# Loading x already transposed through the DMA crossbar instead of transposing it on TensorE

## The chip, the cores and the metric

One core of a Trainium2 chip runs the kernel. The metric is device microseconds (us) from the first to the last instruction of an execution, with the launch's small overhead; "span" is the same without it, as a profile shows it (about 1.8 us less: 289.9 of 291.7 in the profiled run of the kernel before). Each kernel was run several times, beside runs of the kernel before on the same chip. The engines are written as in the profile: PE is TensorE's matmuls, PEld its weight loads, DVE VectorE, ACT ScalarE, POOL GpSimd; SPq and ACTq are the queues on which SyncE and ScalarE issue transfers (the "sync queue" and the "second queue" below).

## The reference

x is 2048 x 512 in bf16. The result mixes a sliding-window attention (32 heads of 16, window 256) and a gated feed-forward block (inner size 1376), with a sigmoid gate per row.

```python
x = A_x
g = sigmoid((x * gate_w).sum(-1, keepdims=True))
a = attention(x @ wqkv, window=256) @ wo      # 32 heads of 16, causal, banded
b = (silu(x @ w1) * (x @ w3)) @ w2
return g * a + (1 - g) * b
```

Every product that contracts over the 512 columns of x needs x with those columns on the partitions, that is, x transposed (`xT` below).

## The kernel before

x is loaded in four pieces of 512 rows, row-major, and TensorE transposes it in 128x128 blocks into PSUM; ScalarE and VectorE take turns to copy the blocks out.

```python
def x_dma(t):
    xs = xp.tile([P, 4, D], BF16, name="xs")
    nc.sync.dma_start(out=xs[:], in_=x2d[512 * t:512 * (t + 1), :].rearrange("(m p) d -> p m d", p=P))
    xs_tiles[t] = xs

x_dma(0); w_dma(D, 2 * D); w_dma(0, D); x_dma(1); w_dma(2 * D, 3 * D)    # K, Q, V weights
...
def x_transposes(m2):                       # 256 rows
    tx = gen.tile([P, 2, NDC, P], BF16, name="g")
    for j in range(2):
        ...
        for c in range(NDC):
            nc.tensor.transpose(out=tx[:, j, c, :], in_=xs[:, m % 4, c * P:(c + 1) * P], identity=ident[:])
    dst = xT[:, :, 2 * m2 * P:(2 * m2 + 2) * P].rearrange("p c (j t) -> p j c t", j=2)
    if m2 % 2 == 0:
        nc.scalar.copy(out=dst, in_=tx[:])
    else:
        nc.vector.tensor_copy(out=dst, in_=tx[:])
```

TensorE's order is fixed by the program. There are 92 "score bursts" (score matmuls for one block, then exp on ScalarE). Units with a fixed place (`must`) follow a burst, and feed-forward units fill the rest of a time budget, which is kept in estimated microseconds:

```python
COST = {"proj": 0.87, "v": 0.87, "tx": 0.45, "gate": 0.4, "up": 0.87, "down": 2.38, "out": 0.87, "pv": 1.22}
...
must[0] += [("v", proj_v, (0,)), ("v", proj_v, (1,)), ("tx", x_transposes, (2,)), ("tx", x_transposes, (3,))]
...
def run(unit):
    kind, fn, args = unit
    done[0] += COST.get(kind, 0)
    fn(*args)
...
for n, (fn, c, a) in enumerate(bursts):
    fn(c, a)                                         # scores and exp
    before = done[0] - carry
    for unit in early: run(unit)                     # projections, transposes, gate
    while (n >= FFN_FROM and ffn_i[0] < len(up_down) and done[0] + lc - before < QUANTUM - 0.4):
        run_ffn()                                    # feed-forward as filler
    carry = min(done[0] + lc - before - QUANTUM, CARRY)
    for unit in late: ...                            # attention output, projection out
```

Here `lc` is the cost of the burst's `late` units, and `carry` hands what a burst overran its `QUANTUM` by to the next one, at most `CARRY` (1.0).

The softmax here doesn't subtract the row's maximum and nothing guards it: scores larger than these inputs give would overflow.

Of the kernel before, what the change touches and what calls it, by code (L numbers as in the profile page):

```python
# [7 lines left out]
ALU = mybir.AluOpType  # L8
ACT = mybir.ActivationFunctionType
BF16 = mybir.dt.bfloat16  # L10
# [5 lines left out]
P = 128  # L16
# [3 lines left out]
def kernel(  # L20
# [12 lines left out]
    nc = tc.nc  # L33
    x2d = A_x.flatten_outer_dims()
    out2d = out.flatten_outer_dims()
    S, D = x2d.shape
# [4 lines left out]
    NDC = D // P  # L41
# [8 lines left out]
    pp = ctx.enter_context(tc.tile_pool(name="pp", bufs=1))  # L50
    xT = pp.tile([P, NDC, S], BF16, name="xT")
# [1 line left out]
    OT = pp.tile([P, NDC, S], BF16, name="OT")  # L53
    gq = pp.tile([P, NT], F32, name="gq")
    omg = pp.tile([P, NT], F32, name="omg")
    ident = pp.tile([P, P], BF16, name="ident")
    wo_sb = pp.tile([P, NDC, D], BF16, name="wo_sb")
    w2_sb = pp.tile([P, NFC, D], BF16, name="w2_sb")
    bsb = pp.tile([P, NT, D], BF16, name="bsb")
# [3 lines left out]
    wqkv_sb = pp.tile([P, NDC, 3 * D], BF16, name="wqkv_sb")  # L63
# [1 line left out]
    eo = pp.tile([P, 4], F32, name="eo")  # L65
    maskEO = pp.tile([P, 2], F32, name="maskEO")

    xp = ctx.enter_context(tc.tile_pool(name="xp", bufs=2))
    qkpool = ctx.enter_context(tc.tile_pool(name="qk", bufs=2))
    dmpool = ctx.enter_context(tc.tile_pool(name="edm", bufs=5))  # L70
    efpool = ctx.enter_context(tc.tile_pool(name="ef", bufs=3))
# [5 lines left out]
    ssml = ctx.enter_context(tc.tile_pool(name="ssml", bufs=2, space=bass.MemoryType.PSUM))  # L77
    gen = ctx.enter_context(tc.tile_pool(name="gen", bufs=3, space=bass.MemoryType.PSUM))

    xs_tiles = {}  # L80

    def x_dma(t):
        xs = xp.tile([P, 4, D], BF16, name="xs")
        nc.sync.dma_start(out=xs[:],
                          in_=x2d[512 * t:512 * (t + 1), :].rearrange("(m p) d -> p m d", p=P))
        xs_tiles[t] = xs

    def w_dma(lo, hi):
        nc.sync.dma_start(out=wqkv_sb[:, :, lo:hi],
                          in_=A_wqkv[:, lo:hi].rearrange("(c p) f -> p c f", p=P))  # L90

    x_dma(0)
    w_dma(D, 2 * D)
    w_dma(0, D)
    x_dma(1)
    w_dma(2 * D, 3 * D)
    nc.gpsimd.dma_start(out=gwc[:], in_=gate_w.rearrange("(c p) -> p c", p=P))

    nc.gpsimd.memset(ident[:], 0.0)
    nc.gpsimd.affine_select(out=ident[:], in_=ident[:], pattern=[[-1, P]],  # L100
                            compare_op=ALU.not_equal, fill=1.0, base=0, channel_multiplier=1)
    nc.gpsimd.memset(eo[:], 1.0)
    nc.gpsimd.affine_select(out=eo[:], in_=eo[:], pattern=[[-2 * DH, 4]],
                            compare_op=ALU.is_ge, fill=0.0, base=0, channel_multiplier=1)
    nc.gpsimd.affine_select(out=eo[:], in_=eo[:], pattern=[[2 * DH, 4]],
                            compare_op=ALU.is_ge, fill=0.0, base=DH - 1, channel_multiplier=-1)
# [4 lines left out]
    nc.gpsimd.affine_select(out=maskA[:], in_=maskA[:], pattern=[[1, P]],  # L111
                            compare_op=ALU.is_ge, fill=0.0, base=0, channel_multiplier=-1)
    nc.gpsimd.memset(Vaug[:, :, :, DH:DH + 1], 1.0)

    def x_transposes(m2):
        tx = gen.tile([P, 2, NDC, P], BF16, name="g")
        for j in range(2):
            m = 2 * m2 + j
            xs = xs_tiles[m // 4]
            for c in range(NDC):  # L120
                nc.tensor.transpose(out=tx[:, j, c, :], in_=xs[:, m % 4, c * P:(c + 1) * P],
                                    identity=ident[:])
        dst = xT[:, :, 2 * m2 * P:(2 * m2 + 2) * P].rearrange("p c (j t) -> p j c t", j=2)
        if m2 % 2 == 0:
            nc.scalar.copy(out=dst, in_=tx[:])
        else:
            nc.vector.tensor_copy(out=dst, in_=tx[:])  # L127

    qk_tiles = {}

# [167 lines left out]
    for c in range(NDC):  # L298
        for p in range(NP):
            bursts.append((burst_dm, c, 2 * p))  # L300
            bursts.append((burst_dm, c, 2 * p + 1))
            if p < NP - 1:
# [2 lines left out]
    NB = len(bursts)  # L305

    must = {n: [] for n in range(NB + 40)}
    start = [("tx", x_transposes, (0,)), ("tx", x_transposes, (1,)),
             ("proj", proj, (0, 0, False)), ("proj", proj, (0, 0, True))]
    must[0] += [("v", proj_v, (0,)), ("v", proj_v, (1,)), ("tx", x_transposes, (2,)),  # L310
                ("tx", x_transposes, (3,))]
    must[1] += [("proj", proj, (0, 1, False)), ("proj", proj, (0, 1, True))]
    must[2] += [("v", proj_v, (2,)), ("v", proj_v, (3,)), ("gate", gate, (0,))]
    must[3] += [("v", proj_v, (4,)), ("v", proj_v, (5,)), ("tx", x_transposes, (4,))]
    must[4] += [("tx", x_transposes, (5,)), ("proj", proj, (0, 2, False)),
                ("proj", proj, (0, 2, True))]
    must[6] += [("v", proj_v, (6,)), ("v", proj_v, (7,)), ("gate", gate, (1,))]
    must[8] += [("v", proj_v, (8,)), ("tx", x_transposes, (6,)), ("tx", x_transposes, (7,))]
    must[9] += [("v", proj_v, (9,)), ("proj", proj, (0, 3, False)), ("proj", proj, (0, 3, True))]
    must[11] += [("gate", gate, (2,)), ("v", proj_v, (10,))]  # L320
    must[12] += [("v", proj_v, (11,))]
# [37 lines left out]
    with tc.manual_schedule(engines={mybir.EngineType.PE}):  # L359
        alloc_qk(0)  # L360
        for unit in start:
            run(unit)
        nc.sync.dma_start(out=w1_sb[:], in_=B_w1.rearrange("(c p) f -> p c f", p=P))
        nc.sync.dma_start(out=w3_sb[:], in_=B_w3.rearrange("(c p) f -> p c f", p=P))
        x_dma(2)
        x_dma(3)
        nc.sync.dma_start(out=w2_sb[:, 0:NFC - 1, :],
                          in_=B_w2[0:(NFC - 1) * P, :].rearrange("(f p) n -> p f n", p=P))
# [58 lines left out]
```

## Time and profile before

| | before |
|---|---|
| time, median of 40 runs beside the change | 290.4 us (288.6 to 293.6) |
| first score matmul (profiled run) | 13.23 us |
| last score burst (its first weight load) | 270.0 us |

The busy times of the page, then of each engine in single stretches. In a stretch's line the columns are: its bounds and length, then for PE, PEld, DVE, ACT and POOL the busy time and number of instructions, the granted clock, the busy share of the 16 DMA engines and what they moved.

```profile
span 289.9 us, 7509 instructions
PE 258.9 (89%) x3152; PEld 164.6 (57%) x3184; DVE 186.7 (64%) x398; ACT 213.9 (74%) x297; POOL 71.8 (25%) x125
```

```profile
0.00:13.20 13.20, 5.64 (x24) 2.58 (x25) 2.44 (x5) 2.98 (x3) 4.54 (x13) 1.00 0.82 256
...
100.00:150.00 50.00, 46.76 (x605) 30.99 (x608) 33.26 (x76) 40.98 (x60) 12.01 (x20) 1.00 0.04 8
150.00:200.00 50.00, 46.12 (x575) 30.43 (x577) 33.64 (x76) 42.39 (x61) 14.41 (x24) 1.00 0.05 11
```

After the start TensorE (PE) is busy 46 to 47 of 50 us and holds 55% of the chain of work that ended last (ACT 19%, DVE 14%), so most of the time depends on it. In the first 13.2 us it has only 5.6 us of work. (The clock of 1.00 in that line says nothing: the trace's first clock record begins at 19.3 us, and a matmul of 512 columns took up to 0.63 us before it, 0.38 later.) The timeline of PE in the start (start, length, what; in brackets the idle time before it and what ended it):

```profile
4.44 1.89 PE L121 MATMUL g<-ident,xs 128*128 128x128 bf16 x16 [4.44 <-DMA xs<-in_A_x_dram]
7.20 1.86 PE L142 MATMUL g<-xT,wqkv_sb 128*128 128x512 bf16 x4 [0.88 <-DVE xT L127]
9.79 1.89 PE L142 MATMUL g<-xT,wqkv_sb 128*128 128x512 bf16 x4 [0.72 <-DMA wqkv_sb<-in_A_wqkv_dram]
13.23 0.61 PE L226 MATMUL big<-qz,kt 32*128 32x512 bf16 x3 [1.56 <-DVE qz L147]
```

These are the first 16 transposes, the K projection, the Q projection (which waited for its weights) and the first scores. PE's waits that the change is aimed at, over the whole run (us, times, longest):

```profile
PE g L121 <- DMA xs<-in_A_x_dram: 4.4, 1, 4.4
...
PE g L142 <- DVE xT L127: 2.1, 3, 0.9
...
PE g L142 <- DMA wqkv_sb<-in_A_wqkv_dram: 0.7, 1, 0.7
```

The kernel already has one kind of crossbar transpose: 64 of 128x128 from SBUF for the attention output. Their time on the issuing queue (min/median/max in ns) and to landing:

```profile
L281 SPq DMA_TRANSPOSE OT<-ocur x64: 1094/1222/2152, 25.9 to 275.3; - x64
...
DMA to landing us min/median/max: 2.2/2.3/3.5
```

### The profile page before, as it was taken

What the parts mean: (1) busy time and instruction counts of PE and PEld (TensorE: products, weight loads), DVE (VectorE), ACT (ScalarE), POOL (GpSimd) and SP (SyncE); (2) the same over time, 40 slices, a digit from 0 to 9 for tenths busy, and PEclk for the clock granted to TensorE, in tenths of its full rate; (3) what the DMA queues carried; (4) which work ended last, traced back from release to release, by engine and by line L of the source; (5) the groups of instructions that cost most, each with busy time, mean ns of one, the idle gap of its engine ahead of it and who ended that gap; (6) DMA issues with size and microseconds to landing.
All of it is one profiled execution on the core that took longest, in us unless ns stands there. A gap on an engine that the chain in (4) does not pass through costs nothing.

```text
span 289.9 us, 7509 instructions
## 1 busy us (share of the span) xinstructions
PE 258.9 (89%) x3152; PEld 164.6 (57%) x3184; DVE 186.7 (64%) x398; ACT 213.9 (74%) x297; POOL 71.8 (25%) x125
## 2 busy tenths in 40 slices
PE   2699898899989999899998999988998998999994
PEld 2145565555655656566665655675675446655671
DVE  1148566777776666558668775566578666765783
ACT  3158887968968999778778988887888778868220
POOL 6003331133303333212302333330232213333000
PEclk9999999999999999999999999999999999999999
DMA  6997000000000000000000000000001111111101
GB/s 164 374 384 252 11 2 9 14 9 11 11 2 19 11 7 9 9 9 10 12 7 14 11 11 9 11 3 9 11 14 46 31 40 33 48 48 43 44 9 36
DMA packets 19298, 13.10 MB, mean 45 GB/s; under 512 B 10721, under 2 KB 18241, under 8 KB 19265
## 3 DMA queue, kind: packets, MB, share of 16 engines
q1 hardware_dynamic: 19232, 12.63, 14.1%
q8 instruction: 25, 0.41, 0.6%
q0 software_dynamic: 32, 0.00, 0.3%
q14 instruction: 9, 0.07, 0.1%
HBM read 8.42 MB, written 2.10 MB: 36 GB/s over the span
## 4 chain that ended last, share of the span: by engine, by line
PE 55%; ACT 19%; DVE 14%; issue 8%; DMA 3%; SPq 0%; ACTq 0%
PE g L199 13%; PE g L183 12%; PE g L272 9%; ACT edm L216 8%; DVE edm L232 5%; ACT edm L217 5%; PE g L142 5%; PE big L226 5%; PE g L206 4%; PE g L154 4%; ACT ef L216 4%; DMA wqkv_sb<-in_A_wqkv_dram 3%; PE big L245 2%; DVE hT L191 2%; DVE qz L147 2%
## 5 line engine op out<-in xcount | busy, mean ns | idle before, releaser
L252 POOL TENSOR_SCALAR_AFFINE_SELECT ef<-ef 128x512 bf16<-128x512 bf16 x112 | 67.3, 638 | 194.4 <-ACT ef L216 194.4
L216 ACT ACTIVATE edm<-big 128x1536 bf16<-128x1536 f32 x64 | 90.6, 1416 | 29.2 <-PE sml L226 29.1
L183 PE MATMUL g<-xT,w_sb 128*128 128x256 bf16 (+1 forms) x704 | 86.4, 273 | 5.3 <-DVE hT L191 4.9
L183 PEld LDWEIGHTS <-w_sb 128*128 128x128 bf16 (+1 forms) x704 | 66.7, 100 | 23.7 <-issue 14.6
L232 DVE TENSOR_TENSOR edm<-edm,maskA 128x1024 bf16<-128x1024 bf16 x64 | 44.2, 691 | 47.1 <-ACT edm L217 46.9
L216 ACT ACTIVATE ef<-big 128x1536 bf16<-128x1536 f32 x28 | 40.7, 1455 | 11.0 <-PE sml L245 10.6
L199 PE MATMUL g<-w_sb,hT 128*128 128x512 bf16 (+1 forms) x163 | 40.0, 379 | 2.1 <-DVE hT L191 1.1
L187 ACT ACTIVATE tt<-g 128x256 bf16<-128x256 f32 (+1 forms) x88 | 32.7, 395 | 11.3 <-PE g L183 9.8
L272 PEld LDWEIGHTS <-edm 128*128 128x128 bf16 x992 | 38.3, 96 | 4.5 <-issue 2.6
L272 PE MATMUL g<-Vaug,edm 128*128 128x17 bf16 x992 | 40.5, 170 | 0.0
L272 PE MATMUL g<-Vaug,ef 128*128 128x17 bf16 x448 | 36.8, 171 | 1.6 <-DVE hT L191 1.0
L217 ACT ACTIVATE edm<-sml 128x512 bf16<-128x512 f32 x64 | 37.5, 587 | 0.0
L142 PE MATMUL g<-xT,wqkv_sb 128*128 128x512 bf16 x121 | 33.7, 397 | 4.1 <-DVE xT L127 2.1
L272 PEld LDWEIGHTS <-ef 128*128 128x128 bf16 x448 | 34.9, 96 | 3.4 <-issue 1.3
L199 PEld LDWEIGHTS <-hT 128*128 128x128 bf16 (+1 forms) x176 | 17.0, 98 | 20.0 <-issue 2.3
L226 PE MATMUL big<-qz,kt 32*128 32x512 bf16 x192 | 24.8, 381 | 3.6 <-DVE qz L147 1.6
L226 PE MATMUL sml<-qz,kt 32*128 32x512 bf16 x64 | 24.4, 381 | 0.0
L142 PEld LDWEIGHTS <-wqkv_sb 128*128 128x128 bf16 x128 | 10.9, 99 | 19.5 <-issue 7.3
L275 DVE RECIPROCAL rden<-g 128x16 f32<-128x16 f32 x32 | 8.2, 257 | 20.4 <-PE g L272 20.1
L154 PE MATMUL g<-wqkv_sb,xT 128*128 128x512 bf16 x55 | 16.8, 417 | 1.1 <-DVE hT L191 0.7
L217 ACT ACTIVATE ef<-sml 128x512 bf16<-128x512 f32 x28 | 16.8, 601 | 0.0
L206 PE MATMUL g<-wo_sb,OT 128*128 128x512 bf16 x61 | 16.2, 381 | 0.2
(214 smaller groups left out, 231.7 us busy)
## 6 DMA issues: line engine op xcount, KB each, us to landing
w_sb<-in_B_w_dram SPq DMA_DIRECT2D x2, 1376.0 KB, 14.0
xs<-in_A_x_dram SPq DMA_DIRECT2D x4, 512.0 KB, 8.0
out_dram<-ot SPq DMA_DIRECT2D x16, 128.0 KB, 1.7
wqkv_sb<-in_A_wqkv_dram SPq DMA_DIRECT2D x3, 512.0 KB, 7.9
w_sb<-in_B_w_dram SPq DMA_DIRECT2D x1, 1280.0 KB, 14.6
OT<-ocur SPq DMA_TRANSPOSE x64, 2.3
wo_sb<-in_A_wo_dram SPq DMA_DIRECT2D x1, 512.0 KB, 7.6
w_sb<-in_B_w_dram SPq DMA_DIRECT2D x1, 96.0 KB, 7.1
```

The costliest lines, as they stand in the source:

```text
L142: nc.tensor.matmul(ps[:], lhsT=wqkv_sb[:, dc, col0:col0 + P], rhs=xT[:, dc, t0:t1], start=(dc == 0), stop=(dc == NDC - 1))
L154: nc.tensor.matmul(ps[:], lhsT=xT[:, c, m * P:(m + 1) * P], rhs=wqkv_sb[:, c, 2 * D:3 * D], start=(c == 0), stop=(c == NDC - 1))
L183: nc.tensor.matmul(gu[0:fs, wch, :], lhsT=wsb[:, dc, f * P:f * P + fs], rhs=xT[:, dc, t * 256:(t + 1) * 256], start=(dc == 0), stop=(dc == ...
L187: nc.scalar.activation(out=tt[0:fs, :], in_=gu[0:fs, 0, :], func=ACT.Tanh, scale=0.5)
L199: nc.tensor.matmul(ps[:], lhsT=hT[0:fs, f, (m % 2) * P:(m % 2 + 1) * P], rhs=w2_sb[0:fs, f, :], start=(f == 0), stop=(f == NFC - 1))
L206: nc.tensor.matmul(ps[:], lhsT=OT[:, c, m * P:(m + 1) * P], rhs=wo_sb[:, c, :], start=(c == 0), stop=(c == NDC - 1))
L216: nc.scalar.activation(out=dst[:, 0:3, 0:w], in_=big[:, :, 0:w], func=ACT.Exp, scale=SCALE)
L217: nc.scalar.activation(out=dst[:, 3, 0:w], in_=sml[:, 0:w], func=ACT.Exp, scale=SCALE)
L226: nc.tensor.matmul(dst, lhsT=kt[32 * u:32 * u + 32, kb * P:(kb + 1) * P], rhs=qz[32 * u:32 * u + 32, :, kb * P:kb * P + n], start=True, st ...
L232: nc.vector.tensor_tensor(out=tri, in0=tri, in1=maskA[:, None, None, :].to_broadcast([P, 4, 2, P]), op=ALU.mult)
L252: nc.gpsimd.affine_select(out=tri, in_=tri, pattern=[[0, 4], [-1, P]], compare_op=ALU.is_ge, fill=0.0, base=-1, channel_multiplier=1)
L272: nc.tensor.matmul(pva[:, k, h8, :], lhsT=lhsT, rhs=Vaug[:, kp, 8 * c + h8, :], start=(bi == 0), stop=(bi == len(blocks) - 1))
```

## The change

The intent is to take 64 transposes off TensorE and eight evacuations off ScalarE and VectorE, and to bring only the first 128 columns of the K and Q weights first, on a second DMA queue. The V weights go to that queue too.

```diff
     def x_dma(t):
-        xs = xp.tile([P, 4, D], BF16, name="xs")
-        nc.sync.dma_start(out=xs[:], ...)
-        xs_tiles[t] = xs
+        for c in range(NDC):
+            nc.sync.dma_start_transpose(out=xT[:, c, 512 * t:512 * (t + 1)],
+                                        in_=x2d[512 * t:512 * (t + 1), c * P:(c + 1) * P])
...
+    w_dma(nc.scalar, D, D + P)
+    w_dma(nc.scalar, 0, P)
     x_dma(0)
-    w_dma(D, 2 * D)
-    w_dma(0, D)
+    w_dma(nc.scalar, 2 * D, 3 * D)
     x_dma(1)
-    w_dma(2 * D, 3 * D)
+    w_dma(nc.sync, D + P, 2 * D)
+    w_dma(nc.sync, P, D)
...
-    def x_transposes(m2): ...               # and ident, the xs tiles
-    start = [("tx", x_transposes, (0,)), ("tx", x_transposes, (1,)),
+    start = [
              ("proj", proj, (0, 0, False)), ("proj", proj, (0, 0, True))]
-    must[0] += [("v", proj_v, (0,)), ("v", proj_v, (1,)), ("tx", x_transposes, (2,)), ("tx", x_transposes, (3,))]
+    must[0] += [("v", proj_v, (0,)), ("v", proj_v, (1,))]
...                                          # likewise the other four "tx" units of must[3], must[4], must[8]
```

After it, w1, w3 and then x(2), x(3) are issued on the sync queue, as before.

More of the change, by code (lines that the diff above doesn't have):

```diff
@@ L55 @@
     omg = pp.tile([P, NT], F32, name="omg")
-    ident = pp.tile([P, P], BF16, name="ident")
     wo_sb = pp.tile([P, NDC, D], BF16, name="wo_sb")
@@ L66 @@
     maskEO = pp.tile([P, 2], F32, name="maskEO")
-    xp = ctx.enter_context(tc.tile_pool(name="xp", bufs=2))
     qkpool = ctx.enter_context(tc.tile_pool(name="qk", bufs=2))
@@ L78, with w_dma @@
     gen = ctx.enter_context(tc.tile_pool(name="gen", bufs=3, space=bass.MemoryType.PSUM))
-    xs_tiles = {}
     def x_dma(t):
-        xs = xp.tile([P, 4, D], BF16, name="xs")
-        nc.sync.dma_start(out=xs[:],
-                          in_=x2d[512 * t:512 * (t + 1), :].rearrange("(m p) d -> p m d", p=P))
-        xs_tiles[t] = xs
-    def w_dma(lo, hi):
-        nc.sync.dma_start(out=wqkv_sb[:, :, lo:hi],
-                          in_=A_wqkv[:, lo:hi].rearrange("(c p) f -> p c f", p=P))
+        for c in range(NDC):
+            nc.sync.dma_start_transpose(out=xT[:, c, 512 * t:512 * (t + 1)],
+                                        in_=x2d[512 * t:512 * (t + 1), c * P:(c + 1) * P])
+    def w_dma(eng, lo, hi):
+        eng.dma_start(out=wqkv_sb[:, :, lo:hi],
+                      in_=A_wqkv[:, lo:hi].rearrange("(c p) f -> p c f", p=P))
+    w_dma(nc.scalar, D, D + P)
+    w_dma(nc.scalar, 0, P)
     x_dma(0)
-    w_dma(D, 2 * D)
-    w_dma(0, D)
+    w_dma(nc.scalar, 2 * D, 3 * D)
     x_dma(1)
-    w_dma(2 * D, 3 * D)
+    w_dma(nc.sync, D + P, 2 * D)
+    w_dma(nc.sync, P, D)
     nc.gpsimd.dma_start(out=gwc[:], in_=gate_w.rearrange("(c p) -> p c", p=P))
-    nc.gpsimd.memset(ident[:], 0.0)
-    nc.gpsimd.affine_select(out=ident[:], in_=ident[:], pattern=[[-1, P]],
-                            compare_op=ALU.not_equal, fill=1.0, base=0, channel_multiplier=1)
     nc.gpsimd.memset(eo[:], 1.0)
@@ L113 @@
     nc.gpsimd.memset(Vaug[:, :, :, DH:DH + 1], 1.0)
-    def x_transposes(m2):
-        tx = gen.tile([P, 2, NDC, P], BF16, name="g")
-        for j in range(2):
-            m = 2 * m2 + j
-            xs = xs_tiles[m // 4]
-            for c in range(NDC):
-                nc.tensor.transpose(out=tx[:, j, c, :], in_=xs[:, m % 4, c * P:(c + 1) * P],
-                                    identity=ident[:])
-        dst = xT[:, :, 2 * m2 * P:(2 * m2 + 2) * P].rearrange("p c (j t) -> p j c t", j=2)
-        if m2 % 2 == 0:
-            nc.scalar.copy(out=dst, in_=tx[:])
-        else:
-            nc.vector.tensor_copy(out=dst, in_=tx[:])
     qk_tiles = {}
@@ L307 @@
     must = {n: [] for n in range(NB + 40)}
-    start = [("tx", x_transposes, (0,)), ("tx", x_transposes, (1,)),
+    start = [
              ("proj", proj, (0, 0, False)), ("proj", proj, (0, 0, True))]
-    must[0] += [("v", proj_v, (0,)), ("v", proj_v, (1,)), ("tx", x_transposes, (2,)),
-                ("tx", x_transposes, (3,))]
+    must[0] += [("v", proj_v, (0,)), ("v", proj_v, (1,))]
     must[1] += [("proj", proj, (0, 1, False)), ("proj", proj, (0, 1, True))]
     must[2] += [("v", proj_v, (2,)), ("v", proj_v, (3,)), ("gate", gate, (0,))]
-    must[3] += [("v", proj_v, (4,)), ("v", proj_v, (5,)), ("tx", x_transposes, (4,))]
-    must[4] += [("tx", x_transposes, (5,)), ("proj", proj, (0, 2, False)),
+    must[3] += [("v", proj_v, (4,)), ("v", proj_v, (5,))]
+    must[4] += [("proj", proj, (0, 2, False)),
                 ("proj", proj, (0, 2, True))]
     must[6] += [("v", proj_v, (6,)), ("v", proj_v, (7,)), ("gate", gate, (1,))]
-    must[8] += [("v", proj_v, (8,)), ("tx", x_transposes, (6,)), ("tx", x_transposes, (7,))]
+    must[8] += [("v", proj_v, (8,))]
     must[9] += [("v", proj_v, (9,)), ("proj", proj, (0, 3, False)), ("proj", proj, (0, 3, True))]
```

## The prediction

> **What bounds the kernel now.** After the start, TensorE: from 50 to 250 us (busy time by stretch) PE is busy 46 to 47 of every 50 us, ScalarE 39 to 42, VectorE 33 to 35. So PE work removed counts nearly in full, and so does any delay of the start. The first 13.2 us hold only 5.6 us of PE work: x lands at 4.4, 16 cold transposes and two evacuations take until 7.2, K projection, wait for Q weights until 9.8, Q projection, qz; first scores at 13.23 (timeline). From 7 to 26 us weights fill the DMA engines (350 to 400 GB/s).
>
> **Removed.** 64 TensorE transposes: 1.9 us per 16 cold (two groups), 1.05 per 16 warm (two groups), 5.9 us of PE. PE's waits for the evacuation of xT: 2.1 us (list of waits). ScalarE loses 4 copies of 1.01 us, VectorE 4 of 0.69; neither binds. The 0.7 us wait for Q weights should go.
>
> **Added.** 16 crossbar transposes of 512x128 (128 KB), all on the sync queue, in order. The trace has only 128x128 ones from SBUF: 1.22 us of queue time each, 2.3 to landing. Their packet records: all 128 data packets (256 B) run in 0.25 us, 1.4 us after the issue's start; the next burst follows 1.27 us later. So most of 1.22 us looks fixed. I estimate 1.8 us for a four times longer one (1.3 if fixed, 4.5 if proportional). The Trainium skill (DMA: Bandwidth & Descriptors, "Latency and other measured facts") gives 261 GB/s for transposes, hence 0.5 us for 128 KB by estimate; the packets agree that moving is not the cost, the issue is.
>
> **Schedule at 1.8 us.** x(0) lands at 0.8+4*1.8+1.1 = 9 us instead of 4.4; K, Q and qz take 5.3; first scores at 14.4 (+1.2). x(1) lands at 16, in time. K/Q rest, w1, w3 follow; x(2) is issued from about 20 us, behind 3.5 MB of weights on full engines, and lands near 29. Its projection (29.2 before, 27.3 with the work removed) waits 1 to 2 us. x(3) lands near 37, needed at 41; w2 near 43, needed at 82. Sum: +1.2 late start, +1.7 wait for x(2), -4.0 for the 48 later transposes, -1.3 evacuation waits: about -2 us. The uncertain term is the issue time: at 1.3 us the sum is -6, at 3 about +13 (x(0) at 14, waits for x(1), x(2)), at 4.5 +30. This is skewed upwards, so I name the time of before.
>
> **Predicted: 290 us, 8 in 10 between 283 and 306. Faster by over 2%: 0.2; within 2%: 0.5; slower: 0.3.**
>
> **What would show it.** Issues by line: xT transposes at 1.5 to 2.2 us of queue time each. Timeline: first scores between 13 and 16 us. PE's waits: on DMA of xT before the first K projection (until about 9 us) and 1 to 2 us before block 2's K projection; none on VectorE's copy of xT. Stretches from 50 us on: PE still busy 46 to 47 of 50. PE busy total down 6 us.
>
> **What would make it wrong.** Issue time proportional to rows: then x(1), x(2), x(3) each stall PE, and the output transposes queued behind them fill their three buffers. Transposes slowed by weight traffic. A fixed issue time: then 284 or below. The feed-forward fill is reordered (the transposes' cost leaves its budget), worth a microsecond or two either way.

## The result and the profile after

The changed kernel takes 290.7 us (median of 20 runs, 290.3 to 292.5) against 290.4 us before. The ratio is 1.0018, with a 95% interval of 0.9997 to 1.0039: the same time. A ratio here is the mean time of one kernel's runs over that of the other's of the same rounds, so it is not quite the ratio of the medians. In the text, "0.75% faster" means a ratio of 0.9925 against the kernel before.

The page of the changed kernel, the same stretches, and PE's timeline of the first 28 us:

```profile
span 289.5 us, 7380 instructions
PE 252.1 (87%) x3089; PEld 158.9 (55%) x3120; DVE 181.4 (63%) x394; ACT 208.3 (72%) x293; POOL 71.4 (25%) x123
```

```profile
0.00:13.20 13.20, 3.73 (x8) 1.15 (x9) 0.91 (x3) 1.71 (x2) 4.15 (x11) 1.00 0.79 145
...
100.00:150.00 50.00, 45.66 (x599) 30.38 (x602) 32.35 (x75) 38.86 (x59) 12.01 (x20) 1.00 0.04 9
150.00:200.00 50.00, 45.57 (x568) 30.13 (x571) 31.47 (x71) 40.53 (x58) 14.41 (x24) 1.00 0.05 10
```

```profile
4.99 0.58 PE L122 MATMUL g<-xT,wqkv_sb 128*128 128x512 bf16 x1 [4.99 <-DMA xT<-in_A_x_dram]
9.17 3.15 PE L122 MATMUL g<-xT,wqkv_sb 128*128 128x512 bf16 x7 [3.59 <-DMA xT<-in_A_x_dram]
14.30 0.39 PE L206 MATMUL big<-qz,kt 32*128 32x512 bf16 x3 [1.99 <-DVE qz L127]
...
24.91 0.89 PE L122 MATMUL g<-xT,wqkv_sb 128*128 128x512 bf16 x2 [0.18 <-DMA xT<-in_A_x_dram]
27.37 1.62 PE L122 MATMUL g<-xT,wqkv_sb 128*128 128x512 bf16 x6 [1.58 <-DMA xT<-in_A_x_dram]
```

PE did lose 6.8 us of work (258.9 to 252.1), and yet the span is the same. (Either trace lacks some 30 matmul records, as the counts of matmuls and of weight loads show, so the difference is fair and the totals are a little low.) The first column block of x(0) lands at 5 us, but the rest only at 9.17, so the first scores come at 14.30, a microsecond later than before. At 25 us PE stands still twice for x(2), 1.8 us in all. The issue, which the prediction held to be the cost, is cheap in the median (min/median/max in ns):

```profile
L80 SPq DMA_TRANSPOSE xT<-in_A_x_dram x16: 1214/1262/4021, 0.8 to 28.7; - x16
...
DMA to landing us min/median/max: 2.7/4.3/11.4
```

A transpose of 128 KB took the queue 1.26 us, against 1.22 us for one of 32 KB. Landing varies from 2.7 to 11.4 us. The issue was not cheap throughout: behind w1 and w3 the four of x(2) held the queue for 4.02, 3.15, 1.27 and 2.17 us, and the mean of all 16 is 1.64 us. The chain that ended last runs through the first two of these and the landing of the third, up to the matmul at 27.37 (start, length, what):

```profile
13.49 4.02 SPq L80
17.55 3.15 SPq L80
20.75 6.58 DMA xT<-in_A_x_dram
```

One more delay had not been foreseen. ScalarE's activation table was loaded at 0.81 us before, ahead of its first copy of xT. That copy is gone, so the load now precedes the first `qz`, behind a wait for a mask:

```profile
11.48 1.28 ACT L125 ACT_TABLE_LOAD   x1 [11.48 <-DVE maskEO L101]
12.78 0.69 ACT L125 ACTIVATE qz<-g,maskEO 128x512 bf16<-128x512 f32 x1
```

The Q projection ends at 12.32 (9.17 + 3.15), so this costs 0.46 us of the start.

Next, the order of work. The table counts in the traces when a score burst starts and how many weight loads of the feed-forward block PE had done by then (880 in all; one up unit is 8 loads).

| burst | before: start, loads done | after: start, loads done |
|---|---|---|
| 12 | 50.63, 24 | 48.81, 40 |
| 48 | 149.31, 362 | 149.41, 386 |
| 91 (last) | 270.00, 802 | 273.06, 842 |

The removed transposes no longer count in the fill budget, so feed-forward work runs ahead by 16 to 40 loads in this table; the attention, whose bursts stand behind that work, is late by 3 us at its end, and only 38 loads are left to fill the time after the last burst instead of 78.

### The profile page after: what moved, and what is told of

The parts are those of the page before. It is cut to its first block, busy times and chain, and to the rows that moved or that the text cites. A ratio compares the mean times of both kernels' runs of the same rounds, so it can differ in the third digit from the quotient of the medians.

```text
span 289.5 us, 7380 instructions
## 1 busy us (share of the span) xinstructions
PE 252.1 (87%) x3089; PEld 158.9 (55%) x3120; DVE 181.4 (63%) x394; ACT 208.3 (72%) x293; POOL 71.4 (25%) x123
## 4 chain that ended last, share of the span: by engine, by line
PE 50%; ACT 16%; DVE 14%; issue 9%; SPq 7%; DMA 2%; ACTq 0%
PE g L179 13%; PE g L252 11%; PE g L163 8%; ACT edm L196 7%; SPq L80 6%; ACT edm L197 6%; DVE edm L212 6%; PE g L122 5%; PE big L206 4%; PE g L186 4%; DVE hT L171 3%; DMA xT<-in_A_x_dram 2%; PE g L134 2%; ACT ef L196 2%; PE big L225 2%
## 5 line engine op out<-in xcount | busy, mean ns | idle before, releaser
L163 PE MATMUL g<-xT,w_sb 128*128 128x256 bf16 (+1 forms) x704 | 87.4, 273 | 5.2 <-DVE hT L171 4.9
L122 PE MATMUL g<-xT,wqkv_sb 128*128 128x512 bf16 x121 | 34.5, 396 | 12.7 <-DMA xT<-in_A_x_dram 10.3
L129 DVE CAST kt<-g 128x512 bf16<-128x512 f32 x16 | 11.0, 685 | 13.0 <-PE g L122 12.9
L181 DVE TENSOR_SCALAR bsb<-g,omg 128x512 bf16<-128x512 f32 x16 | 12.0, 749 | 10.0 <-PE g L179 9.9
```

Source lines behind the costliest of these rows:

```text
L122: nc.tensor.matmul(ps[:], lhsT=wqkv_sb[:, dc, col0:col0 + P], rhs=xT[:, dc, t0:t1], start=(dc == 0), stop=(dc == NDC - 1))
L163: nc.tensor.matmul(gu[0:fs, wch, :], lhsT=wsb[:, dc, f * P:f * P + fs], rhs=xT[:, dc, t * 256:(t + 1) * 256], start=(dc == 0), stop=(dc == ...
```

## The experiments

Theory A: the arithmetic of the start was about right (a gain of some 2 us), and the fill order took it back. The rival B: the order of the fill is worth nothing, and the late start and the waits for x(2) cost all of the gain. The experiments on the start then ask what delays x(0) and what the waits are worth.

### Keeping the budget, transposes gone

```diff
+    NOP = ("tx", lambda: None, ())
+    start = [NOP, NOP, ("proj", ...
     must[0] += [("v", proj_v, (0,)), ("v", proj_v, (1,))]   # + NOP, NOP; likewise in must[3], must[4], must[8]
```

> The changed kernel with the removed transposes' cost (0.45 each) still counted in the fill budget by empty units, so that feed-forward work stands between the same score bursts as in the kernel before. Theory A (the start's net gain of about 3 us survives until 250 us and is lost in the tail, because the missing 3.6 us of budget lets the fill run ahead, puts the last burst 3 us later and leaves too little filler behind it): 1% below both kernels, about 287.5 us, the last score burst at about 267 us with about 113 us of feed-forward work done instead of 118. Rival B (order of the fill is worth nothing; the gain was eaten by the late start and by more waiting in the middle): within 0.3% of the changed kernel, 290.5.

Measured: 288.7 us, ratio 0.9925 (0.9898 to 0.9953). The changed kernel's ratio was 1.0018, so the budget alone is worth 0.9%, 2.7 us. The last burst starts at 267.3, with 802 loads done, as in the kernel before.

### The kernel before with the budget of the changed one

```diff
-    COST = {... "tx": 0.45, ...}
+    COST = {... "tx": 0.0, ...}
```

> The kernel before, unchanged but for the cost of a transpose in the fill budget, set from 0.45 to 0: the fill runs ahead as in the changed kernel, transposes stay on TensorE. Theory A: about 1% slower than before, 293 us, last score burst about 3 us later than 270. Rival B: same time as before, 290.

Measured: 293.3 us, ratio 1.0082 (1.0044 to 1.0120). The same reordering costs the kernel before 2.4 us, with all transposes still on TensorE. The last burst starts at 274.7 with 842 loads done. Theory A is confirmed from both sides; B falls. The four kernels form a square: with the old order the change is worth 0.75% (1 to 0.9925), with the new one 0.64% (1.0082 to 1.0018), so within the noise the two effects add. Nor does the recorded clock explain it: among the runs of these rounds with a recorded clock of 1.0, the budget run took 287.9 to 288.3 us, the kernel before 290.0 to 290.9, and this one 291.8 to 293.4.

Where it is lost is shown by the last 30 us of each kernel: before, after, the change with the budget kept, and before without the cost, in this order.

```profile
259.90:289.90 30.00, 25.45 (x249) 15.84 (x249) 19.14 (x38) 10.21 (x18) 2.40 (x4) 0.98 0.11 33
```

```profile
259.50:289.50 30.00, 24.00 (x282) 14.66 (x283) 17.38 (x35) 12.61 (x19) 4.80 (x8) 0.99 0.14 43
```

```profile
257.00:287.00 30.00, 25.80 (x252) 15.97 (x250) 19.31 (x38) 10.45 (x19) 2.39 (x4) 1.00 0.11 33
```

```profile
261.40:291.40 30.00, 23.94 (x284) 14.62 (x282) 17.17 (x35) 12.61 (x19) 4.80 (x8) 0.99 0.14 43
```

PE is busy 25.5 and 25.8 us where the budget holds the transposes' cost, 24.0 and 23.9 where it doesn't, so the two without it stand idle some 1.5 to 1.9 us more at the end. That is most of the 2.4 to 2.7 us; where the remainder lies the busy times don't resolve. The filler that is missing there can be counted. These are the weight loads of the up projection after the last burst, before and after (number, min/median/max ns, first and last start):

```profile
L183 PEld LDWEIGHTS <-w_sb x56: 96/98/123, 273.2 to 279.2; 128*128 128x128 bf16 x48, 128*96 128x96 bf16 x8
```

```profile
L163 PEld LDWEIGHTS <-w_sb x16: 95/109/123, 273.3 to 275.7; 128*128 128x128 bf16 x8, 128*96 128x96 bf16 x8
```

Seven up units follow the last burst before, two after.

### The kernel before with a larger cost

```diff
-    COST = {... "tx": 0.45, ...}
+    COST = {... "tx": 0.9, ...}
```

> The kernel before with the transposes' cost in the budget raised from 0.45 to 0.9. Theory A (the less feed-forward work is spent before the last score burst, the better the tail is filled, and 0.45 was not the best): 1 to 2 us faster than before, last burst near 267. Rival B (0.45 is where the tail is just filled): no gain; the last burst comes earlier but feed-forward work is left over at the end, so the same 290.

Measured: 290.3 us, ratio 1.0025 (0.9984 to 1.0066). As a test of the budget it says nothing: the cap on `carry` swallows the larger cost, and in the two traces every engine has the same instructions in the same order (PE by its weight loads). It serves as a control instead: a ratio of 1.0025 came from no change at all, so steps of that size below mean nothing. Its profiled run has a span of 286.7 us, against 289.9 for the same program above, and its timeline shows why:

```profile
7.38 3.29 PE L142 MATMUL g<-xT,wqkv_sb 128*128 128x512 bf16 x8 [0.88 <-DVE xT L127]
12.23 0.40 PE L226 MATMUL big<-qz,kt 32*128 32x512 bf16 x3 [1.56 <-DVE qz L147]
...
12.56 1.90 PE L154 MATMUL g<-wqkv_sb,xT 128*128 128x512 bf16 x8
```

The eight matmuls of L154 take 1.90 us here; in the profile above they began at 13.78 and took 3.59 us. The clock records of the two traces say the same: full clock from 10.4 us here, from 19.3 us there. The Trainium skill ("TensorE: Matmul & The Clock Gate", "What's actually happening") describes a free-running window of about 3.4 us in which PE must be busy before a half-rate clock is released; the recorded stretches at half clock inside these runs last 3.41 us, in agreement. So one trace of each kernel can't size a difference of 3 us in the start. My first reading of the two profiles, that the changed kernel leads by 3 us until 250 us, was of that kind: in the control, burst 4 (counted from 0) starts at 24.18, in the changed kernel at 24.33. Sizes below come from the timed rounds.

### V weights behind x(0)

```diff
-    w_dma(nc.scalar, 2 * D, 3 * D)
+    w_dma(nc.sync, 2 * D, 3 * D)          # on the sync queue, after the transposes of x(0)
```

> The changed kernel with the V weights (512 KB) issued on the sync queue behind the four transposes of x(0) instead of on the second queue beside them. Theory A (x(0) lands at 9.2 us because its packets share the DMA engines with the V weights, not because of the issue, which took 1.26 us each and ended at 5.9): x(0) lands near 7 us, first scores near 12.3 instead of 14.3, total about 2 us shorter, 288.7. Rival B (the first transposes from DRAM are slow by themselves): x(0) still lands near 9, no gain.

Measured: 292.4 us, ratio 1.0053 (1.0028 to 1.0077). The part about the cause holds: x(0) is complete by 7.7 us and the first scores run at 11.98 instead of 14.30. So the V weights on "another queue" did slow x(0) down: as the Trainium skill says ("DMA: Bandwidth & Descriptors", "Issuing engines are not separate DMA queues"), both queues run on the same 16 DMA engines. The part about the time does not hold; there was no gain. PE's timeline and clock row (tenths of full clock in 40 slices):

```profile
11.98 0.39 PE L206 MATMUL big<-qz,kt 32*128 32x512 bf16 x3 [1.99 <-DVE qz L127]
...
27.02 2.72 PE L122 MATMUL g<-xT,wqkv_sb 128*128 128x512 bf16 x6 [1.67 <-DMA xT<-in_A_x_dram]
```

```profile
PEclk9988999999999999999999999999999999999999
```

PE now waits longer for x(2), which still lands at 27.0 behind w1 and w3. And after the waits it ran at half clock from 13.6 to 17.0 and from 27.3 to 30.7 us, so that the six matmuls took 2.72 us instead of 1.62. All six timed runs show a granted clock of 0.986 to 0.994.

### x(2) before the big weights

```diff
     x_dma(1)
+    x_dma(2)
     w_dma(nc.sync, D + P, 2 * D)
...
-        x_dma(2)
         x_dma(3)
```

> The changed kernel with the transposes of x(2) issued before the rest of the K and Q weights and w1, w3. Theory A (2.2 us of PE waiting for x(2) between 24.4 and 27.4 us are on the critical path): that wait disappears, total about 2 us shorter, 288.7; w1 and w3 land some 3 us later but before 29 us. Rival B (the wait is made up later, as PE has other slack): within 0.3% of the changed kernel.

Measured: 292.9 us, ratio 1.0066 (1.0037 to 1.0095). The wait for x(2) is gone and another has taken its place:

```profile
PE g L164 <- DMA w_sb<-in_B_w_dram: 0.9, 1, 0.9
```

The feed-forward unit that the shortened budget put at 28 us waits for its weights, which now land later. Burst 6 starts at 31.40, in the changed kernel at 31.43. Neither theory had expected a loss; five of the six runs have a clock of 0.993 or 0.994, so part of it is likely the clock again, which I did not separate.

### One transpose for four

```diff
-        for c in range(NDC):
-            nc.sync.dma_start_transpose(out=xT[:, c, 512 * t:512 * (t + 1)],
-                                        in_=x2d[512 * t:512 * (t + 1), c * P:(c + 1) * P])
+        nc.sync.dma_start_transpose(out=xT[:, :, 512 * t:512 * (t + 1)], in_=x2d[512 * t:512 * (t + 1), :])
```

> The changed kernel with one transpose instruction for 512 rows x 512 columns of x instead of four of 512x128. Theory A (the queue's time is a fixed 1.2 to 1.3 us per instruction, as 128x128 and 512x128 both took it): 1.3 us for each of four instructions, x(2) issued some 15 us earlier in queue time, PE's wait for x(2) gone. Rival B (the time goes by columns or data, and 512x128 matched 128x128 only because the row count is free): 4 to 5 us for each instruction, the start as in the changed kernel. Total time within 1% of the changed kernel in both, as x(0) still shares the engines with the V weights.

Measured: 289.4 us, ratio 0.9983 (0.9946 to 1.0020), the result correct. The first instruction, 512 KB, held the queue from 0.81 to 2.23 us, so 1.42 us. The next one held it for 7.03 us, while the first one's data was still moving:

```profile
2.27 7.03 SPq L79 DMA_TRANSPOSE xT<-in_A_x_dram  x1
```

The last two held it for 9.78 and 3.59 us, so theory A's 1.3 us for each came true for the first only. With nothing backed up the time hardly grew with the size, 1.22, 1.26 and 1.42 us for 32, 128 and 512 KB (the last from a single instruction); that the queue waits while earlier transfers are backed up fits the other three, but was not tested apart. x(0) was complete at 8.41 us, hardly earlier: so its data, next to the V weights, set the time and not the issue. PE still waited for x(2), 1.08 us instead of 1.8, so that part of theory A's expectation failed: the transposes of x(2), too, queued behind the weights. The ratio of 0.9983 is at best a small gain.

### The edits together

The diffs are those above, applied together: first the budget with x(2) early, then all three, then all three with a warm start, whose own diff stands below.

> The changed kernel with two of the three edits: budget kept and x(2) before the rest of K/Q, w1 and w3; the V weights stay on the second queue. Theory A (x(2) early alone gave nothing only because the feed-forward then waited for w3 at 28.8 to 29.7 us; with the budget that work is needed only from about 33 us): about 1 to 2 us below the budget alone, near 287. Rival B (x(2) early is worth nothing): 288.7 as with the budget alone.

Measured: 287.2 us, ratio 0.9898 (0.9848 to 0.9947). The two edits together lie 0.3% below the budget alone; the intervals overlap, so this direction is likely but not sure.

> The changed kernel with the three edits together: transposes' cost kept in the fill budget, V weights behind x(0), x(2) before the rest of K/Q and w1, w3. Theory A (each wait only exposed the next one: with x(0) early PE waited for x(2), with x(2) early it waited for w3, and the budget moves the need for w1, w3 from 29 to 34 us): all gains show together, first scores near 12 us, no DMA wait after that, 284 to 286 us. Rival B (the budget is all there is to gain; the start is limited by something else): as with the budget alone, 288.7.

Measured: 284.9 us, ratio 0.9831 (0.9797 to 0.9865). PE's matmuls wait for no DMA after the first projection. The V weights' place, which alone gained nothing, is worth about 0.7% (0.9898 to 0.9831) once x(2) and the feed-forward weights are no longer the next thing to wait for. (The two come from different rounds and their intervals just overlap; their runs, 286.3 to 287.5 and 284.8 to 285.2 us, do not.) Each wait of the changed kernel stood in front of the next one.

```diff
+    nc.vector.memset(warm[:], 0.0)
+    nc.scalar.activation(out=wact[:], in_=warm[:, 0:4], func=ACT.Exp, scale=1.0)    # early table load
...
+        for _ in range(11):
+            nc.tensor.matmul(wps[:], lhsT=warm[:, 0:P], rhs=warm[:], start=True, stop=True)
```

> The combined kernel with 11 dummy 128x512 matmuls on zeros before the first projection and an early dummy Exp for the table load. Theory A (the low granted clock in the records before about 12 us and in single stretches of 3.4 us after PE waited costs K, Q and V projections up to 2 us each time): full clock from 6 to 8 us on, 1 to 3 us less than the combined kernel, and less spread between runs. Rival B (the clock in the start doesn't matter, the start is bound by data): same as the combined kernel.

Measured: 284.4 us, ratio 0.9810 (0.9770 to 0.9849): no clear gain over the combined kernel, and a wider spread instead of a narrower one (282.9 to 285.7 us). The clock is full from 4.7 us, the first scores run at 10.29, and by burst 4 the kernel leads the combined one by 3.0 us (19.93 against 22.97). Then it waits, and runs at half clock from 32.0 to 35.5:

```profile
PE g L168 <- DMA w_sb<-in_B_w_dram: 3.1, 2, 2.9
```

### Big weights before the rest of K and Q

```diff
     x_dma(2)
-    w_dma(nc.sync, D + P, 2 * D)
-    w_dma(nc.sync, P, D)
...                                          # w1, w3
         x_dma(3)
+        w_dma(nc.sync, D + P, 2 * D)
+        w_dma(nc.sync, P, D)
```

> The combined kernel with the dummy matmuls, and the rest of the K and Q weights issued after x(3) instead of before w1 and w3. Theory A (the warm start was worth 3 us until 27 us, first scores at 10.3 instead of 11.8, and lost it again waiting 3 us for w1 and in a stretch of 3.4 us at half clock after that wait): no wait for w1, 281 to 283 us. Rival B (w1 lands no earlier, or another wait takes its place): 284.4 as before this edit.

Measured: 281.5 us, ratio 0.9705 (0.9659 to 0.9750), correct. PE's matmuls no longer wait for any DMA, and its busy times show a filled start:

```profile
0.00:13.20 13.20, 10.38 (x38) 3.78 (x39) 3.38 (x8) 4.67 (x6) 4.13 (x11) 1.00 0.67 140
13.20:29.20 16.00, 15.53 (x199) 8.48 (x198) 11.87 (x24) 14.54 (x20) 4.79 (x8) 1.00 0.90 245
```

(Of the 10.38 us in the first line, 4.87 are the dummy matmuls.) This version beats both kernels by about 3%. Its clock was lower than 0.998 in one of six runs, the warm start's in five, so the gain over the latter holds the missing stretch at half clock as well as the missing wait.

### The kernel before with a warm start

The edit of the warm start above, with 8 dummy matmuls instead of 11, in the kernel before:

> The kernel before with 8 dummy 128x512 matmuls before the first transpose and the early table load. Theory A (the cold clock costs the kernel before as well, two transpose groups at 1.9 instead of 1.05 us, projections at half rate, but the first Q projection still waits for its weights until 9.8 us): about 2 to 3 us faster than before, so the dummy matmuls explain part of the combined kernel's lead. Rival B (start bound by weights' landing alone): no gain.

Measured: 289.1 us, ratio 0.9970 (0.9921 to 1.0020): no clear gain. The transposes and the K projection run at full rate, then PE waits for the Q weights, and the V projection is at half clock again:

```profile
9.28 1.04 PE L146 MATMUL g<-xT,wqkv_sb 128*128 128x512 bf16 x4 [1.71 <-DMA wqkv_sb<-in_A_wqkv_dram]
...
12.43 3.06 PE L158 MATMUL g<-wqkv_sb,xT 128*128 128x512 bf16 x8
```

So the lead of the best version isn't the dummy matmuls by themselves. Whether the kernel before, with its loads put in the same careful order, would come as far is left open; it was not run.

## Why the prediction was right, and where it wasn't

- **The time, 290 us, same.** Right: 290.7 us, ratio 1.0018.
- **The sum of the start, about -2 us.** Supported by the budget run: with the fill order of before, the change is 0.75% faster, 2.2 us. The single traces can't confirm each term, as the clock's phase alone moved the same program by 3 us.
- **The fill, "worth a microsecond or two either way".** Named as a risk, left out of the sum, and mis-sized: it cost 2.7 us (2.4 in the opposite test), as much as the whole gain. This term is why the total came to zero and not to -2. The named value of 290 allowed for a slow issue instead, which did not happen, so it was right for another reason than the one given: by luck.
- **Issue time, 1.8 us.** Wrong for x(0): 1.26 us, the "fixed" case, for which the prediction promised -6 us. That failed because the issue was not what x(0) waited for. The issues of x(0) ended by 5.9 us; the data, sharing the engines with the V weights, was complete only at 9.17. For x(2) the named risk "transposes slowed by weight traffic" came true: up to 4.02 us, and 1.64 in the mean of all 16.
- **x(0) at 9 us, first scores at 14.4.** The values are right (9.17 and 14.30), the mechanism is not: a shorter issue, a longer landing and a late table load of 0.46 us made up the same number, by luck too.
- **x(1) in time, x(2) waited for 1 to 2 us.** Right: no wait for x before the projections at 16.8 us, 1.8 us at 25 to 27, although x(2) was issued from 13.49 us and not from 20, and its slow issues and late landing took up most of that. But that wait's value was not what its length says: removing it alone gained nothing, as the next weights were late then.
- **Signs in the profile.** No wait for a copy of xT is left, PE's busy total fell by 6.8 us (6 predicted), and PE stays near 46 us of 50 in the middle (45.6 to 47.1).

## What to carry to other kernels

When a kernel's order is made by a budget of estimated costs, taking work out also moves all the filler: keep the old cost in the budget first, and judge the removal and the reordering apart. A start is a chain of waits, each hiding the next, so a single repair may show nothing or even a loss; list what each consumer needs and when, and order the loads by that. Time repeated runs before believing a difference of a few microseconds between two traces, since TensorE's clock at the start can differ that much for the same program.

## What the Trainium skill lacked or had wrong

- "DMA: Bandwidth & Descriptors", "DMA Transpose (X-bar)": the section gives no time on the issuing queue (the page's only figure, in its part on another chip, is a count of sequencer cycles for small tiles of earlier generations). The runs show 1.22, 1.26 and 1.42 us for 32, 128 and 512 KB with nothing backed up, up to 4.0 us for 128 KB behind weight loads, and 3.6 to 9.8 us for 512 KB behind earlier transfers.
- "Advanced Engine Details and Errata", "X-Bar Transpose (TRN2)": it expects 350 to 400 GB/s and calls transposes as fast as other transfers. From 9 to 10 us of the changed kernel, with only 128 KB transposes from DRAM under way, the engines moved 264 GB/s, and 396 GB/s from 16 to 20 us with plain weight loads alone. The 261 GB/s in "DMA: Bandwidth & Descriptors", "Latency and other measured facts", fits.
- "DMA: Bandwidth & Descriptors", "Rules for kernel authors": it says that a transpose next to ordinary DMAs needs nothing. The results were indeed correct, but the rule has no word on speed: from 4 to 7 us of the changed kernel, transposes and V weights together moved 115 to 143 GB/s, against 264 for transposes alone (above) and 308 for the V weights alone (8 to 9 us of the run with the V weights behind x(0)). That the pairing is the reason is not shown: the kernel before, with plain loads only, also fell to 93 and 51 GB/s between 5 and 7 us.
- "TensorE: Matmul & The Clock Gate", "What's actually happening", calls the ramp less than 1% of a typical span. Here the same program had profiled spans of 286.7 and 289.9 us with full clock from 10.4 and from 19.3 us, a difference of 1.1%.
